# Two layers of gated convolution and MLP, forward and backward: the norm correction one tile behind, and earlier loads in the conv backward

## The chip, the cores and the metric

The kernel runs on one core of one Trainium2 chip. The metric is the device time of one execution in microseconds, less is better. In a profile, PE is TensorE, PEld its weight loads, DVE is VectorE, ACT is ScalarE, POOL is GpSimd and SP is SyncE; a "q" behind the name (SPq, POOLq) is the engine's queue in which it issues DMAs. L1031 is line 1031 of the kernel before.

## The reference

```python
def _A_ref(q, k, v, shift_k, ssm_k, ssm_D):        # gated long convolution
    k_shift = causal 4-tap convolution of k with shift_k
    kv = k_shift * v
    y = irfft(rfft(kv, 2S) * rfft(ssm_k, 2S))[:S]   # long causal convolution, one filter a channel
    return q * (y + kv * ssm_D)

def _B_ref(x, w1, b1, w2, b2):
    return gelu(x @ w1 + b1) @ w2 + b2

x = A_q
x = x + _A_ref(_layernorm(x), A_k, A_v, A_shift_k, A_ssm_k, A_ssm_D)   # layer 0
x = x + _B_ref(_layernorm(x), B_w1, B_b1, B_w2, B_b2)                  # layer 1
x = x + _A_ref(_layernorm(x), ...)                                      # layer 2
x = x + _B_ref(_layernorm(x), ...)                                      # layer 3
# returned: x, and its vjp with grad_out for q, k, v, shift_k, ssm_k, ssm_D, w1, b1, w2, b2
```

S = 2048 tokens, D = 512 channels, F = 1376 hidden units, all arrays in bf16.

## The kernel before, in words

The program has four stages, one behind the other: the conv forward (transforms as matmuls with sine and cosine tables), the MLP forward, the MLP backward, and the conv backward, which is mixed with the weight gradients of the MLP. The norms of the four layers (`n0` to `n3`), the hidden values and their gradients go through DRAM between the stages.

**MLP backward** (`phase_mlp`, `bwd`). The 2048 tokens are four lanes of 512 tokens, each of four token tiles of 128. A lane goes through `b_bwd` (layer 3), `a_bwd` (layer 2), `b_bwd` (layer 1), `a_bwd` (layer 0); so there are eight passes through `b_bwd`. `interleave` writes the four lanes into one program: each `yield` adds to the lane's clock, the lane with the lowest clock goes on, and the lanes start 8 units apart. The framework then places each engine's instructions by its own estimate of when they are ready, with the order of the program as priority; each engine's queue is then worked off strictly in order.

In `b_bwd` a pass first makes `gh = w2T gT` (44 matmuls, L1007), copies it (ScalarE, L1009) and multiplies it with the saved gelu derivative `gpb` (VectorE, L1010). Then for each of four token tiles: 11 matmuls into `gn_ps` (L1023); VectorE sums the product of that tile with the norms into one column (L1026); GpSimd makes a diagonal matrix of the column (L1029); one more matmul adds diagonal times norms to the same PSUM tile (L1031, the correction of the normalisation's backward); VectorE scales and adds the residual gradient to `g_sl` (L1032). The PSUM tile has the tag `oo` with four buffers.

`a_bwd` loads the norms of its own layer (L1044) into a tile of the same tag `n` as `b_bwd` (L1016), of which there are `n_bufs` = 3; then VectorE multiplies norms and gradient (L1053), makes eight sums (L1057, L1059), GpSimd turns these into scales (L1063 to L1066), ScalarE applies them (L1068) and VectorE adds (L1070).

**Conv backward** (`conv_backward`). It is a generator. Each `yield` gives a slack in microseconds, and the main loop puts that much of `weight_grads` (transposes `dw_tp` and matmuls `dw_ps`, sums `b1a` on VectorE) behind it. Everything that the two issue on TensorE and VectorE is kept in the order written (`Ordered`); ScalarE, GpSimd and its DMA queue are placed by the framework. Tiles of a tag reuse its buffers, and a new tile waits for all use of the old one, its stores among it. A pool opened later takes memory of the pools closed before it, and waits for their last use in the same way.

The part that matters begins after the spectra (tag `Sg`, two buffers) have been used: four slices of 512 tokens, each with a load of v (two DMAs, L228) and of ks (L689), two buffers each. For each of four tiles of a slice VectorE multiplies twice, in place: the gradient of v into the ks tile, stored as `out_3` (two DMAs, the second half flipped through `o3B`), and the gradient of the shifted k into `W`. TensorE transposes the latter (`gt_ps`, `gr_ps`), ScalarE copies it to `gksT` and `W[1]`. Then TensorE makes the gradient of k for 16 token tiles (`gk_ps`, 16 matmuls each), ScalarE copies it to `gk_o`, which takes the buffers of v (tag `vb`), four tiles to a store. VectorE makes the gradient of the shift filter: for each of four channel chunks it loads a chunk of k^T (`kTc`, tag `Sg`, L733) and makes eight products with a sum. The next stage, the gradient of the long filter, has matmuls into `gh_ps`, which ScalarE copies to `Wh`.

Of the kernel before, what the change touches and what calls it, by code (L numbers as in the profile page):

```python
# [12 lines left out]
ALU = mybir.AluOpType  # L13
BF16 = mybir.dt.bfloat16
F32 = mybir.dt.float32
I32 = mybir.dt.int32
P = 128
# [606 lines left out]
def conv_backward(ctx, nc, tc, dims, consts, dram, res, aps):  # L624
# [27 lines left out]
    with tc.tile_pool(name="cb_w", bufs=1, side="right", reuse_waits="tile") as wp:  # L652
# [25 lines left out]
        with tc.tile_pool(name="cb_io", bufs=1, side="right", reuse_waits="tile") as io:  # L678
            wdiag = io.tile([P, ND, 4, P], BF16, name="wdiag_b")
            dma(out=wdiag, in_=dram.wdiag)  # L680
            vb0 = io.tile([P, 4, D], BF16, name="vb", tag="vb", bufs=2)
            ksb0 = io.tile([P, 4, D], BF16, name="ksb_b", tag="ksb", bufs=2)
            gT = io.tile([P, ND, S + 16], BF16, name="gksT")
            nc.vector.memset(gT[:, :, S:S + 16], 0.0)
            for i in range(4):
                vb = io.tile([P, 4, D], BF16, name="vb", tag="vb", bufs=2) if i else vb0
                tok_io(nc, vb, v_ap, dram.vB, i, eng=nc.gpsimd)
                ksb = io.tile([P, 4, D], BF16, name="ksb_b", tag="ksb", bufs=2) if i else ksb0
                dma(out=ksb, in_=dram.ks[:, 4 * i:4 * i + 4, :])  # L689
                for h in range(4):  # L690
                    gkv = W[h % 2][:, h // 2, 4 + i, :]
                    tt(out=ksb[:, h, :], in0=gkv, in1=ksb[:, h, :], op=ALU.mult)
                    tt(out=gkv, in0=gkv, in1=vb[:, h, :], op=ALU.mult)
                    ps = psum.tile([P, 2, 512], F32, name="gt_ps", tag="sp", bufs=2)
                    for cc in range(ND):
                        cs = slice(cc * P, (cc + 1) * P)
                        nc.tensor.matmul(ps[:, 0, cs], lhsT=gkv[:, cs], rhs=consts.ident if h < 2 else consts.anti,
                                         start=True, stop=True)
                    if h >= 2:
                        pr = psum.tile([P, 2, 512], F32, name="gr_ps", tag="sp", bufs=2)  # L700
                        for cc in range(ND):
                            cs = slice(cc * P, (cc + 1) * P)
                            nc.tensor.matmul(pr[:, 0, cs], lhsT=gkv[:, cs], rhs=consts.ident, start=True, stop=True)
                        for cc in range(ND):
                            c0 = 256 * (i % 2) + P * (h - 2)
                            nc.scalar.activation(out=W[1][:, cc // 2, 2 * (cc % 2) + i // 2, c0:c0 + P],
                                                 in_=pr[:, 0, cc * P:(cc + 1) * P], func=ACT.Identity)
                    t0 = 512 * i + (P * h if h < 2 else 512 - P * (h - 1))
                    nc.scalar.activation(out=gT[:, :, t0:t0 + P],
                                         in_=ps[:, 0, :].rearrange("p (c t) -> p c t", c=ND), func=ACT.Identity)  # L710
                yield 3.0
                last = tok_io(nc, ksb, out3, dram.o3B, i, store=True, eng=nc.gpsimd)
                if i % 2:
                    with tc.issue_after(last.ins):
                        unflip_rows(nc, aps[f"out_{i // 2}"].flatten_outer_dims(), (dram.o0B, dram.o1B)[i // 2],
                                    eng=nc.gpsimd)
            unflip_rows(nc, out3, dram.o3B, eng=nc.gpsimd)
            for t in range(NT):
                ps = psum.tile([P, 2, 512], F32, name="gk_ps", tag="sp", bufs=2)
                for cc in range(ND):  # L720
                    for j in range(4):
                        nc.tensor.matmul(ps[:, 0, cc * P:(cc + 1) * P], lhsT=gT[:, cc, t * P + j:t * P + j + P],
                                         rhs=wdiag[:, cc, j, :], start=(j == 0), stop=(j == 3))
                if t % 4 == 0:
                    go = io.tile([P, 4, D], BF16, name="gk_o", tag="vb", bufs=2)
                nc.scalar.activation(out=go[:, t % 4, :], in_=ps[:, 0, :], func=ACT.Identity)
                if t % 4 == 3:
                    dma(out=out2[(t - 3) * P:(t + 1) * P, :].rearrange("(t p) d -> p t d", p=P), in_=go)
            gwo = io.tile([P, 2, ND, 4], F32, name="gwo", tag="gwo", bufs=1)
            junk = W[0][:, 0, 0:2, :].rearrange("p a (b d) -> p (a b) d", b=2)  # L730
            for cc in range(ND):
                kc = gyp.tile([P, 8192 // 2], BF16, name="kTc", tag="Sg", bufs=2)[:, 0:4 * 544]
                dma(out=kc, in_=dram.kT[:, cc, :, :].rearrange("p i w -> p (i w)"))  # L733
                kc = kc.rearrange("p (i w) -> p i w", i=4)
                for j in range(4):
                    for half in range(2):
                        if half == 0:
                            g_, k_ = gT[:, cc, 0:S].rearrange("p (i q) -> p i q", i=4)[:, :, 0:256], 16 - j
                        else:
                            g_ = W[1][:, cc // 2, 2 * (cc % 2):2 * (cc % 2) + 2, :].rearrange("p a (b q) -> p (a b) q", b=2)  # L740
                            k_ = 272 + j
                        nc.vector.scalar_tensor_tensor(out=junk, in0=g_, scalar=1.0, in1=kc[:, :, k_:k_ + 256],
                                                       op0=ALU.mult, op1=ALU.mult, accum_out=gwo[:, half, cc, j:j + 1])
                    yield 2.2
            gwb = gyp.tile([P, ND, 4], BF16, name="gwb", tag="gwb", bufs=1)
            tt(out=gwb, in0=gwo[:, 0], in1=gwo[:, 1], op=ALU.add)
# [59 lines left out]
TS = 4  # L806
# [189 lines left out]
def b_bwd(nc, m, g, l, s, ret, rows, load=None):  # L996
# [20 lines left out]
        yield 1.0 * k  # L1017
    go = m.spool.tile([P, TS, D], BF16, name="g_sl", tag=f"x{s}", bufs=1)
    cols = m.small.tile([P, 2, TS], F32, name="bb_cols", tag="bb_cols", bufs=4)
    for t in range(TS):  # L1020
        ps = m.psum.tile([P, D], F32, name="gn_ps", tag="oo", bufs=4)
        for c in range(NFC):
            nc.tensor.matmul(ps, lhsT=gz[:, c, t * P:(t + 1) * P], rhs=w.w1T[:, c, :], start=(c == 0),  # L1023
                             stop=(c == NFC - 1))
        junk = m.small.tile([P, D], BF16, name="bb_junk", tag="bb_junk", bufs=2)
        nc.vector.scalar_tensor_tensor(out=junk, in0=ps, scalar=1.0, in1=n[:, t, :], op0=ALU.mult, op1=ALU.mult,  # L1026
                                       accum_out=cols[:, 0, t:t + 1])
        dg = m.small.tile([P, P], BF16, name="bb_diag", tag="bb_diag", bufs=4)
        nc.gpsimd.tensor_scalar(out=dg, in0=m.ident, scalar1=cols[:, 0, t:t + 1], scalar2=-1.0 / D,  # L1029
                                op0=ALU.mult, op1=ALU.mult)  # L1030
        nc.tensor.matmul(ps, lhsT=dg, rhs=n[:, t, :], start=False, stop=True, skip_group_check=True)  # L1031
        nc.vector.scalar_tensor_tensor(out=go[:, t, :], in0=ps, scalar=m.rstd[l][:, s * TS + t:s * TS + t + 1],  # L1032
                                       in1=g[:, t, :], op0=ALU.mult, op1=ALU.add, accum_out=cols[:, 1, t:t + 1])
        yield 2.5
    ret.append((go, cols[:, 1, :]))


def a_bwd(nc, m, g, sumg, l, s, go, first, ret):
    D = m.D
    sl = slice(s * TS, (s + 1) * TS)  # L1040
    y = m.y[:, sl, :]
    rstd = m.rstd[l][:, sl]
    n = m.spool.tile([P, TS, D], BF16, name="nb_sl", tag="n", bufs=m.n_bufs)
    nc.sync.dma_start(out=n, in_=tok(m.n_d[l], s))  # L1044
    u = m.gpool.tile([P, TS, D], BF16, name="ab_u", tag="ab_u", bufs=2)
    for t in range(TS):
        nc.scalar.activation(out=u[:, t, :], in_=y[:, t, :], func=ACT.Identity, scale=rstd[:, t:t + 1],
# [152 lines left out]
def phase_mlp(ctx, nc, tc, dims, consts, dram, res, aps):  # L1200
# [11 lines left out]
    with ExitStack() as st:  # L1212
# [2 lines left out]
        m.spool = st.enter_context(tc.tile_pool(name="m_s", bufs=1))  # L1215
        m.hpool = st.enter_context(tc.tile_pool(name="m_h", bufs=1))
        m.psum = st.enter_context(tc.tile_pool(name="m_ps", bufs=1, space=bass.MemoryType.PSUM, reuse_waits="tile"))
        m.n_bufs = 3
        m.mhalf = m.small.tile([P, TS], F32, name="mhalf", bufs=1)
        nc.vector.memset(m.mhalf, -0.5)  # L1220
        with tc.tile_pool(name="m_g", bufs=2, reuse_waits="tile") as m.gpool:
# [20 lines left out]
        with tc.tile_pool(name="m_gb", bufs=2, reuse_waits="tile") as m.gpool:  # L1242

            def bwd(s):
# [1 line left out]
                g3 = G3[:, s * TS:(s + 1) * TS, :]  # L1246
                yield from b_bwd(nc, m, g3, 3, s, ret, dram_rows(go_ap, dram.goB, s),
                                 lambda: tok_io(nc, g3, go_ap, dram.goB, s))
                g, sg = ret.pop()
                yield from a_bwd(nc, m, g, sg, 2, s, G1[:, s * TS:(s + 1) * TS, :], True, ret)  # L1250
                ret.pop()
                g1 = G1[:, s * TS:(s + 1) * TS, :]
                yield from b_bwd(nc, m, g1, 1, s, ret, sb_rows(g1))
                g, sg = ret.pop()
                yield from a_bwd(nc, m, g, sg, 0, s, None, False, ret)
                tok_io(nc, ret.pop(), out1, dram.o1B, s, store=True)

            interleave([(s * 8.0, bwd(s)) for s in range(NSL)])
# [66 lines left out]
```

## Time and profile before

| | |
|---|---|
| median of 3 runs | 1016.43 us (1014.85 to 1016.79) |
| profiled execution | 1015.93 us |
| its span in the profile | 1013.8 us, 12809 instructions |
| granted TensorE clock, mean | 0.918 |
| DMA | 177.72 MB, mean 175 GB/s |

Times inside the profile count from the start of the span. Rows of "waits" say which engine and line waited for whom: in total, how often, the longest. Rows in order of time give start, duration, engine, line, operation, output <- input, the count, and in brackets the idle time of the engine ahead of it with what ended it. L55 is the line of the helper that keeps the written order, so there the tile's name says which operation it is. In rows of stretches each engine has its busy time and count, followed by the granted TensorE clock, the mean busy share of the 16 DMA engines, and GB/s.

### The profile page before, as it was taken

What the parts mean: (1) busy time and instruction counts of PE and PEld (TensorE: products, weight loads), DVE (VectorE), ACT (ScalarE), POOL (GpSimd) and SP (SyncE); (2) the same over time, 40 slices, a digit from 0 to 9 for tenths busy, and PEclk for the clock granted to TensorE, in tenths of its full rate; (3) what the DMA queues carried; (4) which work ended last, traced back from release to release, by engine and by line L of the source; (5) the groups of instructions that cost most, each with busy time, mean ns of one, the idle gap of its engine ahead of it and who ended that gap; (6) DMA issues with size and microseconds to landing.
All of it is one profiled execution on the core that took longest, in us unless ns stands there. A gap on an engine that the chain in (4) does not pass through costs nothing.

```text
span 1013.8 us, 12809 instructions
## 1 busy us (share of the span) xinstructions
PE 807.2 (80%) x4677; PEld 411.5 (41%) x4754; DVE 733.2 (72%) x1207; ACT 612.5 (60%) x806; POOL 150.5 (15%) x271
## 2 busy tenths in 40 slices
PE   0678768872777678768998988879899995879998
PEld 0444333340323233323433333335355553655674
DVE  6615529597999999977466567885369993897883
ACT  5735435452889988889724444535465654645664
POOL 5411100002212221100011111221010203310000
PEclk9788979986889898879999999989999998879999
DMA  5076637204365445685895767448256588656231
GB/s 207 22 267 203 259 124 260 83 1 145 112 189 151 131 139 156 200 231 160 265 280 176 214 175 168 146 161 296 109 165 237 200 310 278 186 166 199 89 107 44
DMA packets 153415, 177.72 MB, mean 175 GB/s; under 512 B 50117, under 2 KB 133768, under 8 KB 152712
## 3 DMA queue, kind: packets, MB, share of 16 engines
q1 hardware_dynamic: 141816, 136.75, 43.7%
q0 software_dynamic: 11536, 40.15, 11.0%
q8 instruction: 37, 0.61, 0.3%
q14 instruction: 26, 0.21, 0.1%
HBM read 92.61 MB, written 82.13 MB: 172 GB/s over the span
## 4 chain that ended last, share of the span: by engine, by line
PE 28%; DVE 19%; DMA 11%; ACT 8%; issue 6%; POOL 4%; SPq 1%; ACTq 0%; DVEq 0%; POOLq 0%
PE dw_ps L55 10%; DMA nb_sl<-n_d 3%; DVE ln_st L891 3%; PE gh_ps L1007 3%; PE sp_ps L55 2%; PE dw_tp L55 2%; PE gh_ps L55 2%; PE iv_ps L55 2%; DMA ksb_b<-ks_d 2%; PE gn_ps L1023 2%; DVE g_o L961 2%; DMA tabFb<-tabF_d 2%; POOL bb_diag L1029 2%; DVE bb_junk L1057 2%; ACT g_o L957 1%
## 5 line engine op out<-in xcount | busy, mean ns | idle before, releaser
L55 PE MATMUL dw_ps<-G,dw_tm 128*128 128x512 bf16 x672 | 166.9, 383 | 3.1 <-ACT dw_tm L1121 1.4
L1121 ACT ACTIVATE dw_tm<-dw_tp 128x1024 bf16<-128x1024 bf16 x88 | 89.9, 1024 | 68.3 <-PE dw_tp L55 68.2
L990 PE MATMUL o_ps<-w_sb,h_sl 128*128 128x512 bf16 x343 | 95.7, 422 | 39.9 <-DVE h_sl L960 39.0
L978 PE MATMUL z_ps<-nT_sl,w_sb 128*128 128x512 bf16 x346 | 83.1, 394 | 20.4 <-DMA nT_sl<-n_sl 18.6
L55 PEld LDWEIGHTS <-dw_tm 128*128 128x128 bf16 x704 | 65.3, 99 | 62.2 <-ACT dw_tm L1121 2.1
L1009 ACT ACTIVATE gz_sl<-gh_ps 128x512 bf16<-128x512 f32 x88 | 51.2, 597 | 60.2 <-PE gh_ps L1007 59.2
L1023 PE MATMUL gn_ps<-w1T_sb,gz_sl 128*128 128x512 bf16 x346 | 82.8, 386 | 1.3 <-DVE gz_sl L1010 0.9
L1007 PE MATMUL gh_ps<-gT_sl,w2T_sb 128*128 128x512 bf16 x343 | 82.1, 383 | 0.4
L990 PEld LDWEIGHTS <-h_sl 128*128 128x128 bf16 x352 | 36.4, 107 | 92.9 <-DVE h_sl L960 45.1
L978 PEld LDWEIGHTS <-w_sb 128*128 128x128 bf16 x352 | 35.0, 101 | 73.0 <-DMA nT_sl<-n_sl 27.9
L980 ACT ACTIVATE g_z<-z_ps,b1col 128x512 bf16<-128x512 f32 x88 | 54.1, 690 | 11.3 <-PE z_ps L978 11.3
L55 PEld LDWEIGHTS <-dw_fm 128*128 128x128 bf16 x704 | 48.2, 100 | 21.1 <-issue 1.4
L55 PE MATMUL dw_tp<-ident,dw_fm 128*128 128x128 bf16 x704 | 55.3, 223 | 0.0
L956 ACT ACTIVATE g_s<-g_t 128x2048 bf16<-128x2048 bf16 (+1 forms) x24 | 42.5, 1773 | 18.3 <-DVE g_t L955 18.3
L1023 PEld LDWEIGHTS <-gz_sl 128*128 128x128 bf16 x352 | 34.9, 100 | 43.4 <-issue 3.5
L1007 PEld LDWEIGHTS <-w2T_sb 128*128 128x128 bf16 x352 | 34.6, 98 | 40.3 <-issue 0.8
L55 DVE TENSOR_REDUCE b1a<-dw_fm 128x1 f32<-128x2048 bf16 x22 | 49.6, 2279 | 1.0 <-DMA dw_fm<-gz_d 1.0
L1029 POOL TENSOR_SCALAR bb_diag<-ident,bb_cols 128x128 bf16<-128x128 bf16 x32 | 22.9, 716 | 157.8 <-DVE bb_junk L1026 156.5
L894 POOL TENSOR_SCALAR rstd<-ln_mv 128x4 f32<-128x4 f32 x16 | 11.5, 717 | 232.9 <-DVE ln_mv L892 148.8
L1010 DVE TENSOR_TENSOR gz_sl<-gz_sl,gpb 128x2048 bf16<-128x2048 bf16 (+1 forms) x24 | 27.2, 1135 | 24.3 <-ACT gz_sl L1009 13.5
L1068 ACT ACTIVATE nb_sl<-nb_sl,ab_ab 128x512 bf16<-128x512 bf16 x32 | 24.6, 804 | 33.1 <-DVE bb_junk L1026 22.9
L891 DVE BATCH_NORM_STATS2 ln_st<-x_sl 128x6 f32<-128x512 bf16 x64 | 41.9, 668 | 2.9 <-DMA x_sl<-in_A_q_dram 2.8
(284 smaller groups left out, 1646.0 us busy)
## 6 DMA issues: line engine op xcount, KB each, us to landing
dw_fm<-h_d SPq DMA_DIRECT2D x22, 512.0 KB, 5.1
dw_fm<-gz_d SPq DMA_DIRECT2D x22, 512.0 KB, 4.5
n_d<-n_sl SPq DMA_DIRECT2D x16, 512.0 KB, 3.5
h_d<-h_sl SPq DMA_DIRECT2D x16, 512.0 KB, 2.9
gp_d<-g_p SPq DMA_DIRECT2D x16, 512.0 KB, 3.5
nb_sl<-n_d SPq DMA_DIRECT2D x16, 512.0 KB, 4.6
gpb<-gp_d SPq DMA_DIRECT2D x16, 512.0 KB, 4.8
gz_d<-gz_sl SPq DMA_DIRECT2D x16, 512.0 KB, 4.9
```

Of the source, the lines that this page charges most:

```text
L55: return self.tc.keep_in_program_order(f(*args, **kwargs))
L891: nc.vector.bn_stats(out=st, in_=x[:, t, :])
L956: nc.scalar.activation(out=sg, in_=t, func=ACT.Sigmoid)
L978: nc.tensor.matmul(ps, lhsT=w.w1[:, dc, c * P:(c + 1) * P], rhs=nT[:, dc, :], start=(dc == 0), stop=(dc == ND - 1))
L980: nc.scalar.activation(out=zb[:, c - c0, :], in_=ps, func=ACT.Identity, bias=w.b1col[:, c:c + 1])
L990: nc.tensor.matmul(ps, lhsT=h[:, c, t * P:(t + 1) * P], rhs=w.w2[:, c, :], start=False, stop=(c == NFC - 1))
L1007: nc.tensor.matmul(ps, lhsT=w.w2T[:, dc, c * P:(c + 1) * P], rhs=gT[:, dc, :], start=(dc == 0), stop=(dc == ND - 1))
L1009: nc.scalar.activation(out=gz[:, c, :], in_=ps, func=ACT.Identity)
L1010: nc.vector.tensor_tensor(out=gz[:, c0:c0 + k, :], in0=gz[:, c0:c0 + k, :], in1=gp[:, 0:k, :], op=ALU.mult)
L1023: nc.tensor.matmul(ps, lhsT=gz[:, c, t * P:(t + 1) * P], rhs=w.w1T[:, c, :], start=(c == 0), stop=(c == NFC - 1))
L1029: nc.gpsimd.tensor_scalar(out=dg, in0=m.ident, scalar1=cols[:, 0, t:t + 1], scalar2=-1.0 / D, op0=ALU.mult, op1=ALU.mult)
L1121: nc.scalar.activation(out=dst, in_=ps, func=ACT.Identity)
```

## The change

1. In `b_bwd` the loop over token tiles has one more round. In round t the 11 matmuls of tile t come first, then the correction matmul and `g_sl` of tile t-1, then the sum and the diagonal of tile t. In round 1 `b_bwd` also issues the load of the norms that the following `a_bwd` needs and hands the tile over; `a_bwd` loads nothing. `n_bufs` in the MLP is 4 instead of 3.
2. In the conv backward all four slices' ks and v loads are issued ahead of the slice loop: ks into four buffers, v into two tiles of two slices each in the buffers of the spectra (tag `Sg`). The output tiles of the k gradient take the ks buffers (four) instead of the v buffers (two).
3. All four chunks of k^T are loaded ahead of the matmuls of the k gradient: two into the `Sg` buffers, which hold v until then, and two into parts of `W[0]`.

```diff
@@ conv_backward
-            vb0 = io.tile([P, 4, D], BF16, name="vb", tag="vb", bufs=2)
-            ksb0 = io.tile([P, 4, D], BF16, name="ksb_b", tag="ksb", bufs=2)
+            ksbs = [io.tile([P, 4, D], BF16, name="ksb_b", tag="ksb", bufs=4) for i in range(4)]
+            vbs = []
+            for i in range(4):
+                if i % 2 == 0:
+                    v2 = gyp.tile([P, 2, 4, D], BF16, name="vb", tag="Sg", bufs=2)
+                vbs.append(v2[:, i % 2])
+                dma(out=ksbs[i], in_=dram.ks[:, 4 * i:4 * i + 4, :])
+                tok_io(nc, vbs[i], v_ap, dram.vB, i, eng=nc.gpsimd)
...
             for i in range(4):
-                vb = io.tile([P, 4, D], BF16, name="vb", tag="vb", bufs=2) if i else vb0
-                tok_io(nc, vb, v_ap, dram.vB, i, eng=nc.gpsimd)
-                ksb = io.tile([P, 4, D], BF16, name="ksb_b", tag="ksb", bufs=2) if i else ksb0
-                dma(out=ksb, in_=dram.ks[:, 4 * i:4 * i + 4, :])
+                vb, ksb = vbs[i], ksbs[i]
...
+            w0f = W[0][:, :, :, :].rearrange("p e s d -> p (e s d)")
+            kcs = [gyp.tile([P, 4096], BF16, name="kTc", tag="Sg", bufs=2)[:, 0:4 * 544] for cc in range(2)]
+            kcs += [w0f[:, 2048 + 2176 * x:2048 + 2176 * (x + 1)] for x in range(2)]
+            for cc in range(ND):
+                dma(out=kcs[cc], in_=dram.kT[:, cc, :, :].rearrange("p i w -> p (i w)"))
             unflip_rows(nc, out3, dram.o3B, eng=nc.gpsimd)
...
-                    go = io.tile([P, 4, D], BF16, name="gk_o", tag="vb", bufs=2)
+                    go = io.tile([P, 4, D], BF16, name="gk_o", tag="ksb", bufs=4)
...
-                kc = gyp.tile([P, 8192 // 2], BF16, name="kTc", tag="Sg", bufs=2)[:, 0:4 * 544]
-                dma(out=kc, in_=dram.kT[:, cc, :, :].rearrange("p i w -> p (i w)"))
-                kc = kc.rearrange("p (i w) -> p i w", i=4)
+                kc = kcs[cc].rearrange("p (i w) -> p i w", i=4)
@@ b_bwd
-    for t in range(TS):
-        (11 matmuls; sum; diagonal; correction; g_sl of tile t, as above)
-        yield 2.5
-    ret.append((go, cols[:, 1, :]))
+    pss = {}
+    for t in range(TS + 1):
+        if t < TS:
+            (11 matmuls of tile t into pss[t])
+        if t > 0:
+            u, ps = t - 1, pss.pop(t - 1)
+            nc.tensor.matmul(ps, lhsT=dg, rhs=n[:, u, :], start=False, stop=True, skip_group_check=True)
+            (g_sl of tile u)
+        if t < TS:
+            (sum and diagonal dg of tile t)
+        if t == 1:
+            n2 = m.spool.tile([P, TS, D], BF16, name="nb_sl", tag="n", bufs=m.n_bufs)
+            nc.sync.dma_start(out=n2, in_=tok(m.n_d[l - 1], s))
+        yield 2.5 if t < TS else 0.2
+    ret.append((go, cols[:, 1, :], n2))
@@ a_bwd
-    n = m.spool.tile([P, TS, D], BF16, name="nb_sl", tag="n", bufs=m.n_bufs)
-    nc.sync.dma_start(out=n, in_=tok(m.n_d[l], s))
@@ phase_mlp
-        m.n_bufs = 3
+        m.n_bufs = 4
```

More of the change, by code (lines that the diff above doesn't have):

```diff
@@ L1019, in b_bwd @@
     cols = m.small.tile([P, 2, TS], F32, name="bb_cols", tag="bb_cols", bufs=4)
-    for t in range(TS):
[L1021 to L1033, printed above, removed]
-        yield 2.5
@@ L1035, in b_bwd @@
-    ret.append((go, cols[:, 1, :]))
-def a_bwd(nc, m, g, sumg, l, s, go, first, ret):
+    pss = {}
+    for t in range(TS + 1):
+        if t < TS:
+            ps = pss[t] = m.psum.tile([P, D], F32, name="gn_ps", tag="oo", bufs=4)
+            for c in range(NFC):
+                nc.tensor.matmul(ps, lhsT=gz[:, c, t * P:(t + 1) * P], rhs=w.w1T[:, c, :], start=(c == 0),
+                                 stop=(c == NFC - 1))
+        if t > 0:
+            u, ps = t - 1, pss.pop(t - 1)
+            nc.tensor.matmul(ps, lhsT=dg, rhs=n[:, u, :], start=False, stop=True, skip_group_check=True)
+            nc.vector.scalar_tensor_tensor(out=go[:, u, :], in0=ps, scalar=m.rstd[l][:, s * TS + u:s * TS + u + 1],
+                                           in1=g[:, u, :], op0=ALU.mult, op1=ALU.add, accum_out=cols[:, 1, u:u + 1])
+        if t < TS:
+            junk = m.small.tile([P, D], BF16, name="bb_junk", tag="bb_junk", bufs=2)
+            nc.vector.scalar_tensor_tensor(out=junk, in0=pss[t], scalar=1.0, in1=n[:, t, :], op0=ALU.mult,
+                                           op1=ALU.mult, accum_out=cols[:, 0, t:t + 1])
+            dg = m.small.tile([P, P], BF16, name="bb_diag", tag="bb_diag", bufs=4)
+            nc.gpsimd.tensor_scalar(out=dg, in0=m.ident, scalar1=cols[:, 0, t:t + 1], scalar2=-1.0 / D,
+                                    op0=ALU.mult, op1=ALU.mult)
+        if t == 1:
+            n2 = m.spool.tile([P, TS, D], BF16, name="nb_sl", tag="n", bufs=m.n_bufs)
+            nc.sync.dma_start(out=n2, in_=tok(m.n_d[l - 1], s))
+        yield 2.5 if t < TS else 0.2
@@ L1039, in a_bwd @@
+    ret.append((go, cols[:, 1, :], n2))
+def a_bwd(nc, m, g, sumg, n, l, s, go, first, ret):
     D = m.D
@@ L1248, in bwd @@
                                  lambda: tok_io(nc, g3, go_ap, dram.goB, s))
-                g, sg = ret.pop()
-                yield from a_bwd(nc, m, g, sg, 2, s, G1[:, s * TS:(s + 1) * TS, :], True, ret)
+                g, sg, n = ret.pop()
+                yield from a_bwd(nc, m, g, sg, n, 2, s, G1[:, s * TS:(s + 1) * TS, :], True, ret)
                 ret.pop()
@@ L1253, in bwd @@
                 yield from b_bwd(nc, m, g1, 1, s, ret, sb_rows(g1))
-                g, sg = ret.pop()
-                yield from a_bwd(nc, m, g, sg, 0, s, None, False, ret)
+                g, sg, n = ret.pop()
+                yield from a_bwd(nc, m, g, sg, n, 0, s, None, False, ret)
                 tok_io(nc, ret.pop(), out1, dram.o1B, s, store=True)
```

## The prediction

> **What bounds the kernel now.** I read the page first (busy shares and the 40 slices of 25.3 us), then busy time by stage, then the waits of the stages that the diff touches, and last the order of time in them.
>
> ```profile
> PE 807.2 (80%) x4677; PEld 411.5 (41%) x4754; DVE 733.2 (72%) x1207; ACT 612.5 (60%) x806; POOL 150.5 (15%) x271
> PE   0678768872777678768998988879899995879998
> DVE  6615529597999999977466567885369993897883
> ```
>
> ```profile
> core 0: us, PE busy (x) PEld busy (x) DVE busy (x) ACT busy (x) POOL busy (x), PEclk, DMA share, GB/s
> 495.00:680.00 185.00, 159.12 (x694) 67.56 (x706) 128.90 (x285) 85.77 (x137) 29.44 (x60) 0.97 0.70 201
> ...
> 806.00:870.00 64.00, 50.46 (x378) 29.80 (x384) 44.58 (x65) 34.72 (x63) 15.26 (x22) 0.89 0.80 270
> 870.00:902.00 32.00, 22.93 (x306) 20.77 (x308) 30.20 (x39) 15.21 (x31) 6.55 (x8) 0.84 0.51 161
> 902.00:930.00 28.00, 27.79 (x214) 16.22 (x216) 26.53 (x36) 16.14 (x19) 3.31 (x4) 1.00 0.79 247
> 930.00:1013.00 83.00, 77.89 (x608) 51.71 (x614) 53.30 (x80) 49.12 (x79) 3.71 (x6) 1.00 0.28 84
> ```
>
> TensorE is the engine to watch in all of them. The backward MLP runs from about 495 to 680 us: TensorE idles 25.9 us there and VectorE 56.1. In the conv backward, 806 to 870 and 870 to 902 hold 13.5 and 9.1 us of idle TensorE; 902 to 930 is full, and 930 to the end 94% full. From 806 on TensorE and VectorE run in an order written into the program, and that order is the same after the change. So idle time taken from TensorE there comes off the end, unless VectorE then ends last.
>
> **Part 1: the correction one token tile behind.** The waits between 495 and 697 us (total, times, longest) name the idle time:
>
> ```profile
> PE gn_ps L1031 <- POOL bb_diag L1029: 23.8, 23, 3.4
> ...
> DVE g_sl L1032 <- PE gn_ps L1031: 22.3, 26, 1.5
> ...
> DVE gy_bf L1053 <- DMA nb_sl<-n_d: 7.8, 4, 3.2
> ```
>
> Nearly all of TensorE's idle time, 23.8 of 25.9 us, is before the correction matmul, which needs the VectorE sum of the same token tile and then the GpSimd diagonal. VectorE in turn waits 22.3 us for that matmul. One pass in order of time shows how the two feed each other:
>
> ```profile
> 574.95 0.39 PE L1031 MATMUL gn_ps<-nb_sl,bb_diag 128*128 128x512 bf16 x1 [0.18 <-POOL bb_diag L1029]
> ...
> 575.37 0.95 SPq L1044 DMA_DIRECT2D nb_sl<-n_d  x1
> ...
> 582.47 1.23 DVE L1053 TENSOR_TENSOR gy_bf<-nb_sl,g_sl 128x2048 bf16<-128x2048 bf16 x1 [3.21 <-DMA nb_sl<-n_d]
> ...
> 586.18 0.68 DVE L1026 SCALAR_TENSOR_TENSOR bb_junk<-gn_ps,nb_sl 128x512 bf16<-128x512 f32 x1
> ...
> 586.97 1.02 POOL L1029 TENSOR_SCALAR bb_diag<-ident,bb_cols 128x128 bf16<-128x128 bf16 x1
> ...
> 588.04 0.61 PE L1031 MATMUL gn_ps<-nb_sl,bb_diag 128*128 128x512 bf16 x1 [3.38 <-POOL bb_diag L1029]
> ```
>
> The norms of the next stage are asked for right behind the pass's last correction (574.95 + 0.39, issue at 575.37): that buffer became free only then. They land 7 us later, VectorE stands 3.21 us for them, its queue (the sum at 586.18 among it) is late, and TensorE stands 3.38 us.
>
> After the change the eleven matmuls of the next tile stand between a tile's product and its correction:
>
> ```profile
> 542.81 2.39 PE gn_ps L1023 x11
> ```
>
> The way from sum to correction is 588.04 - 586.18 = 1.86 us in the pass above, where GpSimd took 1.02 us. It fits behind 2.39 us as long as VectorE isn't over 0.5 us late. No instruction is added on TensorE, VectorE or GpSimd; 32 corrections, sums and diagonals move. The last tile of each of eight passes has no own product behind it and relies on other lanes' matmuls; in the last pass there are none. The norm loads keep their number (SyncE, 16 in all) and move from behind the last correction to the second tile, some two tiles or 5 us earlier. SyncE issues in order, so a load that waits for a buffer holds up the transposes and gpb loads behind it. Followed by hand through the interleaved lanes, four buffers give each second-stage load a free slot within about one token tile's time of when it is issued; the first-stage loads wait for the same releases as now. The fourth buffer pays for the earlier load; I cost the queue at nothing, and if it isn't covered it is a rival below.
>
> Bounds: nothing, if the waits only move, and 23.8 us. Below nothing needs a new wait, which is the slower rival. VectorE allows the gain: 22.3 + 7.8 us of its 56.1 idle are these waits. But in the last third it is nearly full (645 to 670 us: 21.0 of 25), so the ends of passes stay. I take 15 us, about two thirds, nearer to the upper row because the chain of 1.9 us is shorter than its new cover.
>
> **Part 2: v, ks and k^T at once.** TensorE and VectorE in order of time:
>
> ```profile
> 850.84 0.59 PE L55 MATMUL dw_ps<-G,dw_tm 128*128 128x512 bf16 x2
> 860.57 0.61 PE L55 MATMUL gt_ps<-ident,Wb 128*128 128x128 bf16 x4 [9.14 <-DVE Wb L55]
> ...
> 868.93 0.61 PE L55 MATMUL gt_ps<-ident,Wb 128*128 128x128 bf16 x8
> ...
> 875.25 9.10 PE L55 MATMUL gk_ps<-wdiag_b,gksT 128*128 128x128 bf16 x160
> 892.70 8.26 PE L55 MATMUL gk_ps<-wdiag_b,gksT 128*128 128x128 bf16 x96 [8.36 <-ACT gk_o L726]
> ```
>
> ```profile
> 859.63 0.42 DVE L55 TENSOR_TENSOR ksb_b<-Wb,ksb_b 128x512 bf16<-128x512 bf16 x1 [16.71 <-DMA ksb_b<-ks_d]
> ...
> 870.48 1.23 DVE L55 SCALAR_TENSOR_TENSOR Wb<-gksT,kTc 128x1024 bf16<-128x1024 bf16 x1 [2.20 <-ACT gksT L709]
> ...
> 926.41 1.23 DVE L55 SCALAR_TENSOR_TENSOR Wb<-Wb,kTc 128x1024 bf16<-128x1024 bf16 x1
> ```
>
> ```profile
> 795.47 0.56 POOL L733 DMA_DIRECT2D kTc<-kT_d  x1 [6.49 <-DVE pr_u L55]
> ...
> 844.58 0.58 POOL L689 DMA_DIRECT2D ksb_b<-ks_d  x1 [1.61 <-DMA o3B_d<-ksb_b]
> ```
>
> ```profile
> 892.06 1.09 ACT L726 ACTIVATE gk_o<-gk_ps 128x512 bf16<-128x512 f32 x2 [8.87 <-DMA out_dram<-gk_o]
> ...
> 935.70 1.09 ACT L780 ACTIVATE Wh<-gh_ps 128x514 bf16<-128x514 f32 x2
> ```
>
> Two gaps go. *Slice 2:* its ks load waits for slice 0's store to land and is issued at 844.58; VectorE waits 16.71 us, TensorE 9.14. With four ks buffers it is issued with the first ones. *The k gradient:* the third output tile waits for the first one's store; TensorE idles 8.36. With four buffers, free once the slices' own stores have landed, this goes too.
>
> The clock adds to it. In stretches of 5 us (columns as above; PEclk is third from the end):
>
> ```profile
> 820.00:825.00 5.00, 4.95 (x37) 2.76 (x36) 4.90 (x7) 2.55 (x3) 0.00 (x0) 1.00 0.47 129
> ...
> 855.00:860.00 5.00, 0.00 (x0) 0.00 (x0) 0.37 (x1) 0.00 (x0) 0.00 (x0) 0.50 0.26 102
> 860.00:865.00 5.00, 3.75 (x26) 2.57 (x27) 4.86 (x9) 3.31 (x10) 1.43 (x2) 0.50 0.39 136
> ...
> 890.00:895.00 5.00, 2.30 (x22) 2.29 (x22) 4.90 (x8) 1.48 (x3) 0.00 (x0) 0.50 0.22 90
> ```
>
> The granted clock is 0.50 after each gap. The last 96 matmuls took 8.26 us; at the rate of the first 160 (9.10 / 160) they take 5.46, so 2.8 us are lost. After the first gap I put 1.7 us: two groups of four transposes took 0.61 each where later one group of eight did, and the gradient matmuls between slices 2 and 3 are slow too. TensorE: 9.14 + 8.36 + 2.8 + 1.7 = 22.0 us. The Trainium skill ("TensorE: Matmul & The Clock Gate", Part 1) agrees on the half clock after an idle window, but has it last about 3.4 us, which would make 1.7 us lost per gap, an estimate 1.1 us under my two terms; the rows decide.
>
> VectorE caps this. It is full from 870 to 930 us, and its shift-filter products read the transposed gradient that TensorE makes in slice 3. That slice starts 868.93 - (9.14 + about 1.4 of clock) = 858.4, so VectorE moves by 10.5 us, not 16.7. Its last product, at 926.41, ends 9.3 - 1.2 = 8.1 us before ScalarE fills the next stage's buffer at 935.70, which I assume lies over that gradient. So the path moves by at most 10.5 + 8.1 = 18.6 us before VectorE ends last, less than 22.0: I take 18.6.
>
> Costs: eight v and four ks loads are only moved in GpSimd's queue. The last load would be issued near 810, instead of 849, and nothing in that queue is due until the first store at 835.8. The DMA must carry 1 MB of ks more before 834; the half-free stretch 820 to 825 (share 0.47) has room for most of it. The Trainium skill ("DMA: Bandwidth & Descriptors", Issuing engines are not separate DMA queues) speaks against a gain from issuing at once: all loads share the same engines. Here the four slices are due 6 us and more apart from 834 on, so sharing costs nothing unless the landing passes 834. k^T loses its early start: its first two loads, now at 795.47 and later, get the buffers that then hold v, so the first can start after slice 1 (about 841) and at worst behind slice 3's stores (about 856). First use is near 860, landings are 4 to 9 us; that costs VectorE 0 to 5 us. I take 2, nearer to the free end since GpSimd is idle after slice 1's stores.
>
> Sum: 15 + 18.6 - 2 = 31.6 us. The profiled execution took 1015.93 us (span 1013.8 and 2.1 around it), 0.5 under the median of 1016.43. 1015.93 - 31.6 = 984.3.
>
> **The rivals.**
> (A) Both parts pay: 984, from 976 to 992 (MLP part 10 to 20, conv part 14 to 19).
> (B) The MLP part pays little: VectorE has 128.9 of 185 us of work in a fixed queue, and a correction that comes later makes the next stage's input later too; the waits move to the sums or to the gz products. With 3 us left of it: 996. For it speaks the dense last third; against it 22.3 + 7.8 us of VectorE waits that have nothing to wait for any more.
> (C) The conv loads pay half: the k^T loads or the stores land late (DMA share near 1.0 around 830 to 850), and VectorE, already full, carries the delay. With 9 us of conv gain: 992.
> (D) Slower: product tiles are held over one more tile, and there are four PSUM buffers for lanes that overlap in pairs; three live tiles a lane would be six. A product that waits for another lane's correction and g_sl costs at least 0.39 + 0.75 us. From 1.0 us on each of 32 tiles it eats the whole 31.6; at 1.5 us the time is 1032, counted as 1015.93 - 31.6 + 48. Against it: no wait of a product for a PSUM buffer stands among today's waits.
> (E) No change: the gaps go, but all move to VectorE's end: 1016.
>
> **How the numbers follow.** A 0.56, B 0.19, C 0.12, D 0.06, E 0.03; 0.04 for more than expected, under 976. The prediction is A's 984. From 973 to 1001 the range leaves out D, E and edges, together about 0.15. A, B, C and the upside are faster: 0.91 less 0.01 for a B that shrinks to nothing. Within 0.2%, which is about what a measurement of this kernel can tell from no change, 0.03; slower 0.07.
>
> **What would show it.** Right: TensorE's wait for the diagonal under 9 us in total; second-stage norm loads issued before the pass's last correction, and no VectorE wait for them; no VectorE wait for ks; 256 k-gradient matmuls in one run of about 14.6 us; the next filter stage 17 us closer to the start of the conv backward. Wrong: a wait of the products for a PSUM tile, of VectorE for k^T, or of TensorE for the norms.

## The result, and the profile after

Median 985.06 us (982.26 to 987.2, four runs) against 1016.61 us for the kernel before (1014.85 to 1021.69, four runs): ratio 0.968, 95% interval 0.9638 to 0.9722. The forecast of 984 is met within 1.1 us, but the two terms behind it are not: the MLP part paid far more than its 15 us and the conv part about half of its 16.6, and the errors cancelled. The profiled execution took 987.2 us, span 985.4.

From the page of the changed kernel, TensorE's row and the 40 slices (of 24.6 us):

```profile
PE 803.6 (82%) x4677; PEld 411.7 (42%) x4754; DVE 729.5 (74%) x1207; ACT 611.6 (62%) x806; POOL 152.5 (15%) x271
...
PE   0686867984378777777899999978999998995998
...
DVE  6624508787899999995847778895369997499873
```

The work is the same (803.6 us of TensorE against 807.2, with equal counts) in a span 28.4 us shorter. Four marks show where it went: the first `gpb` load, the first sine-table matmul (`sp_ps`, right behind the MLP backward), VectorE's first product on `ks`, and the end.

| us | start of MLP backward | its length | middle stage | conv part |
|---|---|---|---|---|
| before | 490.5 | 223.8 | 120.0 | 179.5 |
| after | 496.75 | 198.9 | 118.8 | 171.0 |

The start lies 6 us later although nothing ahead of it was changed; over all kernels below it lies between 489.6 and 498.8, so I count it as chance and compare lengths of stages. They say 25 us in the MLP and 8.5 in the conv part.

**The MLP part.** Busy time by stretches, from the first `gpb` load to the last correction and to the first sine-table matmul (columns: TensorE, its weight loads, VectorE, ScalarE, GpSimd, then clock, DMA share, GB/s). Before:

```profile
490.50:678.10 187.60, 161.72 (x700) 67.97 (x712) 127.24 (x282) 89.12 (x143) 29.44 (x60) 0.98 0.70 203
490.50:714.30 223.80, 191.18 (x902) 84.81 (x917) 146.79 (x312) 107.01 (x163) 34.38 (x67) 0.97 0.71 214
```

After:

```profile
496.75:660.90 164.15, 154.81 (x701) 69.27 (x713) 124.94 (x283) 88.05 (x143) 31.81 (x60) 0.98 0.79 230
496.75:695.60 198.85, 184.84 (x902) 86.42 (x917) 143.35 (x312) 106.05 (x163) 36.74 (x67) 0.97 0.78 238
```

Waits of the changed kernel from 495 to 680 us (total, times, longest):

```profile
DVE g_sl L1036 <- PE gn_ps L1035: 11.7, 6, 3.0
...
DVE gz_sl L1016 <- DMA gpb<-gp_d: 11.4, 5, 5.3
...
PE gn_ps L1035 <- POOL bb_diag L1043: 8.3, 5, 4.0
```

TensorE's wait for the diagonal fell from 23.8 us in 23 waits to 8.3 in 5; two of these five, 2.81 and 4.03 us in the last pass, hold 6.8 of it. No row of VectorE waiting for the norms is left.

And TensorE is *busy* 6.9 us less for the same 700 matmuls (161.72 to 154.81). A part of that is the clock. Before, a wait of 2.72 us that ended at 559.74 and the one of 3.38 us that ended at 588.04 were followed by half clock while TensorE worked without a pause:

```profile
560.50:562.50 2.00, 2.00 (x7) 0.75 (x5) 1.68 (x5) 2.00 (x4) 0.00 (x0) 0.52 0.12 42
588.50:590.50 2.00, 2.00 (x6) 0.70 (x5) 1.81 (x5) 0.99 (x3) 0.00 (x0) 0.50 0.90 268
```

Counting half of the busy time at clock 0.50 as lost, an estimate, the stretch lost 3.5 us to the clock before and 0.9 after. That is 2.7 of the 6.9 us. The other 4.2 are 0.23 us for each of the 18 waits that went, over the wait itself; what makes them up was not tried.

**The conv part.** GpSimd's queue, VectorE, ScalarE and TensorE of the changed kernel in order of time:

```profile
832.92 1.67 POOL L219 DMA_DIRECT2D out_dram<-o1B_d  x1 [0.81 <-issue]
834.58 1.13 POOL L724 DMA_DIRECT2D kTc<-kT_d  x2
840.10 1.05 POOL L724 DMA_DIRECT2D Wb<-kT_d  x2 [4.39 <-PE gt_ps L55]
```

```profile
830.68 0.42 DVE L55 TENSOR_TENSOR ksb_b<-Wb,ksb_b 128x512 bf16<-128x512 bf16 x1
...
850.61 1.23 DVE L55 SCALAR_TENSOR_TENSOR Wb<-gksT,kTc 128x1024 bf16<-128x1024 bf16 x1 [19.05 <-DMA kTc<-kT_d]
...
903.42 1.22 DVE L55 SCALAR_TENSOR_TENSOR Wb<-gksT,Wb 128x1024 bf16<-128x1024 bf16 x1
...
904.69 1.22 DVE L55 SCALAR_TENSOR_TENSOR Wb<-Wb,Wb 128x1024 bf16<-128x1024 bf16 x1
```

```profile
904.74 1.09 ACT L786 ACTIVATE Wh<-gh_ps 128x514 bf16<-128x514 f32 x2 [9.95 <-DVE Wb L55]
```

```profile
845.50 14.46 PE L55 MATMUL gk_ps<-wdiag_b,gksT 128*128 128x128 bf16 x256
...
905.39 8.03 PE L55 MATMUL gh_ps<-tabG,GY 128*128 128x257 bf16 x48 [10.30 <-ACT Wh L786]
```

Both old gaps are gone: no wait for ks, and the 256 matmuls of the k gradient run in one piece of 14.46 us. But k^T is asked for at 834.58, behind all stores of the slices, and is there at 850.61. VectorE stands 19.05 us. The last of its products that reads the transposed gradient in `gksT` is the last but one, at 903.42; ScalarE fills `Wh` as soon as that has ended, at 904.74, and TensorE stands 10.30 us for ScalarE. The 48 matmuls behind that gap take 8.03 us; before, behind a gap of 0.25 us, they took 5.51.

### The profile page after: what moved, and what is told of

It is laid out like the page before. It is cut to its first block, busy times and chain, and to the rows that moved or that the text cites. A ratio compares the mean times of both kernels' runs of the same rounds, so it can differ in the third digit from the quotient of the medians.

```text
span 985.4 us, 12825 instructions
## 1 busy us (share of the span) xinstructions
PE 803.6 (82%) x4677; PEld 411.7 (42%) x4754; DVE 729.5 (74%) x1207; ACT 611.6 (62%) x806; POOL 152.5 (15%) x271
## 4 chain that ended last, share of the span: by engine, by line
PE 38%; DVE 35%; ACT 9%; DMA 7%; issue 5%; POOL 4%; SPq 1%; ACTq 0%; DVEq 0%; POOLq 0%
PE sp_ps L55 8%; PE gh_ps L1013 6%; PE gn_ps L1031 6%; DVE Wb L55 6%; PE dw_ps L55 5%; DVE ln_st L897 3%; PE gh_ps L55 3%; DVE b1a L55 2%; DVE g_o L967 2%; PE iv_ps L55 2%; DMA Hspec_d<-Hg 2%; DMA kTc<-kT_d 2%; DMA tabFb<-tabF_d 2%; DVE pr_u L55 2%; PE dw_tp L55 1%
## 5 line engine op out<-in xcount | busy, mean ns | idle before, releaser
L1031 PE MATMUL gn_ps<-w1T_sb,gz_sl 128*128 128x512 bf16 x345 | 80.7, 379 | 0.6 <-DVE gz_sl L1016 0.3
L1013 PE MATMUL gh_ps<-gT_sl,w2T_sb 128*128 128x512 bf16 x344 | 79.1, 379 | 0.5
L959 ACT ACTIVATE g_q<-g_z 128x2048 bf16<-128x2048 bf16 (+1 forms) x24 | 42.8, 1783 | 0.1
```

The lines of the kernel that those rows point to most:

```text
L959: nc.scalar.activation(out=q, in_=zb, func=ACT.Square)
L1013: nc.tensor.matmul(ps, lhsT=w.w2T[:, dc, c * P:(c + 1) * P], rhs=gT[:, dc, :], start=(dc == 0), stop=(dc == ND - 1))
```

## The experiments

All times are medians; each ratio is to the kernel before, run on the same chip. The three stages are read at the marks of the table above.

**1 and 2: each part by itself.** The first takes `b_bwd`, `a_bwd` and `n_bufs` from the change and `conv_backward` from before; the second the reverse.

> The MLP part alone; the conv backward is as before. Theory (the waits for the diagonal were the whole idle time of that stage and they go): from the first gpb load to the first transform matmul of the conv backward the trace went from 223.8 to 198.9 us, so 1016.5 - 25 = 991.5 us, with TensorE's gaps of 9.1 and 8.4 us in the conv backward back. Rival (the prediction's size, 15 us, and the rest of the trace's difference belongs to the conv part or to chance): 1001 us.

Measured: 992.84 us, ratio 0.9781 [0.9731, 0.983]; MLP backward 199.9, conv part 178.6.

> The conv part alone; the MLP is as before. Theory (the late k^T loads cost most of what the loads and buffers gain): from the first ks product to the end the trace went from 179.5 to 171.0 us, so 1016.5 - 8.5 = 1008 us, VectorE waiting some 19 us for k^T. Rival (the prediction's size, 16.6 us): 1000 us, no wait for k^T above 5 us.

Measured: 1008.15 us, ratio 0.9911 [0.9876, 0.9945]; MLP backward 222.7, conv part 170.4. In its waits VectorE again stands 19.0 us for k^T and TensorE 11.9 for `Wh`:

```profile
DVE Wb L55 <- DMA kTc<-kT_d: 19.0, 1, 19.0
PE gh_ps L55 <- ACT Wh L786: 11.9, 1, 11.9
ACT Wh L786 <- DVE Wb L55: 11.6, 1, 11.6
```

The two parts are independent: 2.2% and 0.9% add up to about the 3.2% of both, and each stage's length in the change is that of the part alone, within 1.1 us.

**3: k^T early.** Three chunks go into the buffer of the output gradient, which is free by then, ahead of the slices.

```diff
+            gyf = res.gy_bf[:, :, :].rearrange("p t d -> p (t d)")
+            kcs = [gyf[:, 2176 * x:2176 * (x + 1)] for x in range(3)] + [w0f[:, 4224:6400]]
+            for cc in range(3):
+                dma(out=kcs[cc], in_=dram.kT[:, cc, :, :].rearrange("p i w -> p (i w)"))
             for i in range(4):          # the slices
...
+            dma(out=kcs[3], in_=dram.kT[:, 3, :, :].rearrange("p i w -> p (i w)"))
```

> The changed kernel with three chunks of k^T loaded ahead of the slices into the buffer of the input gradient (free after the inverse transform), the fourth into W behind slice 3. Theory (VectorE starts the shift filter 8 us late only because of k^T, and its end sets the next stage): VectorE's wait for k^T goes from 19 to about 10 us (then it waits for the transposed gradient), TensorE's gap of 10.3 us before the next stage shrinks to about 2, and the half clock behind it goes: 985 - 10 = 975 us. Rival (the loads come when the DMA is full, so they push others back, or VectorE is bound anyway): 983 us or more.

Measured: 972.31 us (971.17 to 976.52), ratio 0.9579 [0.9539, 0.9618], below the interval of the change. The conv part took 157.6 us, 13.5 less than in the change and 21.9 less than before. Its VectorE, ScalarE and TensorE in order of time:

```profile
836.70 1.23 DVE L55 SCALAR_TENSOR_TENSOR Wb<-gksT,gy_bf 128x1024 bf16<-128x1024 bf16 x1 [7.48 <-ACT gksT L717]
...
891.44 1.22 DVE L55 SCALAR_TENSOR_TENSOR Wb<-Wb,Wb 128x1024 bf16<-128x1024 bf16 x1
```

```profile
891.49 1.09 ACT L787 ACTIVATE Wh<-gh_ps 128x514 bf16<-128x514 f32 x2 [0.73 <-DVE Wb L55]
```

```profile
892.14 5.51 PE L55 MATMUL gh_ps<-tabG,GY 128*128 128x257 bf16 x48 [1.08 <-ACT Wh L787]
```

VectorE now waits for the transposed gradient only, TensorE stands 1.08 us instead of 10.30, and the 48 matmuls are back at 5.51.

**4: ks, v and the output buffers without the k^T loads.** k^T is loaded inside the loop of products, as before, but its `Sg` buffers hold v.

> Conv part without the early k^T: ks and v at once, four output buffers, k^T chunk by chunk as before (two buffers, which now hold v until slice 1 and slice 3 are done); MLP as before. Theory (k^T is late because its buffers hold v and its loads stand behind other DMAs; asking for it in the loop makes it later still): slower than the conv part alone by 0 to 6 us, 1008 to 1014 us. Rival (k^T's place doesn't matter, the gain comes from ks and the output buffers): the same as the conv part alone within 2 us.

Measured: 1024.89 us, ratio 1.0104 [1.0039, 1.0169]; conv part 184.8. It was expected to stay faster than the kernel before and is slower. GpSimd's queue, VectorE's wait, and the stretches behind:

```profile
879.06 0.75 POOL L731 DMA_DIRECT2D out_dram<-gk_o  x1 [2.82 <-ACT gk_o L729]
879.81 1.10 POOL L736 DMA_DIRECT2D kTc<-kT_d  x2
```

```profile
DVE Wb L55 <- DMA kTc<-kT_d: 33.7, 1, 33.7
```

```profile
915.00:930.00 15.00, 7.22 (x50) 4.29 (x51) 14.62 (x21) 3.56 (x4) 2.36 (x3) 0.76 0.82 257
930.00:945.00 15.00, 6.41 (x39) 4.61 (x37) 14.83 (x19) 2.96 (x6) 0.78 (x1) 0.56 0.26 62
```

The load that went out at 795.47 before now stands behind the fourth store of the k gradient. VectorE idles 33.7 us beside work of TensorE and then makes its 32 products; from 915 us on TensorE is half idle beside them. So the freed buffers alone lose; they need k^T moved with them.

**7: only the first chunk early.** As experiment 3, with chunk 0 alone ahead of the slices.

> The changed kernel with the first chunk of k^T alone loaded ahead of the four slices (into the output gradient's buffer, which is free by then); the other three chunks are issued where they were. With three chunks ahead the time was 972.3 us. Theory (only the first chunk's landing at 850.6 us costs, VectorE standing 19 us for it; the later chunks land while the first is multiplied for 9.8 us): VectorE's products begin within 1 us of the transposes' end at about 842, the conv part from the first ks product takes 157 to 160 us, total 971 to 975 us. Rival (the queue is as long for the second chunk: it still lands 15 to 17 us after its issue and VectorE stands for it after the first): a new wait of 3 to 9 us for the second chunk, conv part 162 to 167, total 977 to 982 us.

Measured: 975.69 us, ratio 0.9551 [0.9512, 0.959]; conv part 157.7, as with three chunks. VectorE's first product:

```profile
842.02 1.23 DVE L55 SCALAR_TENSOR_TENSOR Wb<-gksT,gy_bf 128x1024 bf16<-128x1024 bf16 x1 [7.53 <-ACT gksT L714]
```

No wait for the second chunk follows, though it still took 15.4 us from issue to landing. Only the first landing was on the path.

**8: what makes the landing slow.** In the changed kernel, two memory-to-memory copies of 1 MB (the reversed rows of `out_1` and `out_3`) go behind the second and fourth store of the k gradient.

```diff
-                if i % 2:
+                if i == 1:
                     with tc.issue_after(last.ins):
                         unflip_rows(...)
...
-            unflip_rows(nc, out3, dram.o3B, eng=nc.gpsimd)
...
+                    if t in (7, 15):
+                        with tc.issue_after(last.ins):
+                            (unflip_rows of out_1 at t = 7, of out3 at t = 15)
```

> The changed kernel with two memory-to-memory copies, the reversed rows of out_1 and of the third output (1 MB each), moved behind the second and the fourth store of gk; the k^T loads keep their place behind slice 3's stores. Theory (k^T lands 16 us after its issue because those copies fill the DMA engines that it shares): the first chunk lands 6 to 10 us after its issue, VectorE waits 6 to 11 us for it instead of 19, conv part 161 to 165 us against 171, total 975 to 980 us. Rival (the stores of the slices and the other stage's loads alone keep the engines full): landing 14 us or more, VectorE waits 15 us or more, total 983 to 987 us.

Measured: 978.28 us, ratio 0.9572 [0.9522, 0.9622]; conv part 163.6. The issue and the first product:

```profile
833.37 1.12 POOL L724 DMA_DIRECT2D kTc<-kT_d  x2
```

```profile
844.84 1.23 DVE L55 SCALAR_TENSOR_TENSOR Wb<-gksT,kTc 128x1024 bf16<-128x1024 bf16 x1 [12.01 <-DMA kTc<-kT_d]
```

The two `Sg` loads landed 11.8 us after issue (median) instead of 16.4, which is still later than the 6 to 10 us expected, and VectorE's wait is 1 us above its range; conv part and total lie in theirs. In experiment 4 the same loads, issued when little else ran, took 4.7 (median of four). So the traffic beside them sets the landing, the copies some 4.6 us of it; how the rest divides between the slices' stores and the other stage's loads was not tried. Of the 13.5 us of conv part between the change and experiment 3, 7.4 go with the copies; how the other 6.1 divide between the late issue and the other traffic was not tried either. This split rests on one profiled execution of each kernel: the ratios of experiments 3 and 8 (0.9579 and 0.9572) do not tell the two apart.

**5: the lag alone.** Round loop of the change, norms loaded in `a_bwd` as before, three buffers, conv part as before.

> The kernel before with the lag alone: the correction's diagonal matmul and the add run one token tile behind, norms loaded where they were (three buffers), convolution backward as before. MLP stage alone with both parts took 199.9 us from the first gpb load to the first sine-table matmul, 223.8 before. Theory (the lag covers the waits of TensorE for the diagonal and is most of the gain): stage 204 to 209 us, TensorE's wait for the diagonal below 10 us against 23, VectorE's wait for the norms still 7 to 12 us, total 998 to 1003 us. Rival (the two parts need each other: without the diagonal's wait the kernel only comes earlier to norms that are not there): VectorE's wait for the norms grows to 15 us or more, stage 213 or more, total 1008 us.

Measured: 1022.51 us, ratio 1.004 [1.0013, 1.0068]; MLP backward 231.8 in the profiled execution, 8 us *more* than before. That execution took 1028.16 us, the longest of ten; the ratio puts the loss at some 4 us (1.3 to 6.9). The rival named the wait that grows, but its 1008 us was too low. The waits from 495 to 680 us, and one pass in order of time:

```profile
PE gn_ps L1029 <- POOL bb_diag L1037: 23.8, 6, 8.3
DVE gy_bf L1058 <- DMA nb_sl<-n_d: 17.7, 4, 7.6
...
DVE ab_p L1058 <- DMA nb_sl<-n_d: 4.0, 2, 3.4
```

```profile
533.08 0.38 PE L1029 MATMUL gn_ps<-nb_sl,bb_diag 128*128 128x512 bf16 x1
...
535.21 0.41 SPq L1049 DMA_DIRECT2D nb_sl<-n_d  x1
...
541.88 1.22 DVE L1058 TENSOR_TENSOR gy_bf<-nb_sl,g_sl 128x2048 bf16<-128x2048 bf16 x1 [7.63 <-DMA nb_sl<-n_d]
...
545.60 0.68 DVE L1034 SCALAR_TENSOR_TENSOR bb_junk<-gn_ps,nb_sl 128x512 bf16<-128x512 f32 x1
...
546.46 0.37 POOL L1037 TENSOR_SCALAR bb_diag<-ident,bb_cols 128x128 bf16<-128x128 bf16 x1 [0.19 <-DVE bb_junk L1034]
...
546.89 0.61 PE L1029 MATMUL gn_ps<-nb_sl,bb_diag 128*128 128x512 bf16 x1 [8.26 <-POOL bb_diag L1037]
```

The last correction at 533.08 frees the norms' buffer, the next norms are asked for at 535.21 and used at 541.88; VectorE stands 7.63 us for them. In its queue the other lane's sum (545.60) lies behind, so that lane's diagonal is late and TensorE stands 8.26 us. A lag of one tile, 2.4 us, cannot cover that. It also makes the last correction later, and so the load: the total wait for norms from 495 to 680 us rose from 9.4 to 21.7 us.

Up to the last correction of the stage TensorE waits 31.7 us for the diagonal, in eight waits only; before it was 23.8 in 23. The stretch:

```profile
496.30:693.40 197.10, 164.52 (x715) 71.11 (x713) 126.53 (x283) 89.55 (x143) 25.64 (x60) 0.92 0.68 195
```

With a third of the waits TensorE is busier than before (161.72), at a clock of 0.92 instead of 0.98. By the estimate used above, 9.2 us of this stretch are lost to half clock, and the rest, 155.3, lies close to that of the change (154.0). So a few long waits cost more here than many short ones.

**6: the norms alone.** Loaded a stage ahead, four buffers, correction in its old place.

> The kernel before with the norms alone: loaded a stage ahead into four buffers, correction in its old place, convolution backward as before. Theory (two separate waits, the norms' being the smaller): VectorE's wait for the norms goes, TensorE's wait for the diagonal stays at 20 us or more, stage 215 to 219 us against 223.8, total 1008 to 1012 us. Rival (the norms' wait is covered by the diagonal's, and is worth nothing by itself): stage 222 or more, total 1015 to 1018 us.

Measured: 1013.45 us, ratio 0.9944 [0.9916, 0.9971]; MLP backward 219.7, 4 us less than before. Its waits from 495 to 680 us:

```profile
DVE g_sl L1032 <- PE gn_ps L1031: 22.5, 27, 1.0
PE gn_ps L1031 <- POOL bb_diag L1029: 21.0, 24, 2.6
```

Norms are never waited for, and the short way from sum to diagonal to correction stays open on 26 of 32 tiles (23.8 us up to the last correction at 683.42). So the waits before had two sources: the short way behind most tiles, and a load in another lane behind some long ones. In stage lengths of the profiled executions the lag alone costs 8 us and the early norms alone bring 4; together they bring 24 (experiment 1). By the ratios it is 0.4% slower, 0.6% faster and 2.2% faster.

**9 and 10: the place or the buffer.** Experiment 5 with `n_bufs` 4, the loads left in `a_bwd`; and the changed kernel with `n_bufs` 3.

> The kernel before with the lag and a fourth norms buffer; the loads stay at the head of the second stage, convolution backward as before. The lag alone took 231.8 us for the MLP stage, with VectorE waiting 21.7 us for norms whose load goes out only once the pass's last correction, now a tile later, has released its buffer. Theory (the buffer's release is what makes that load late): with a free buffer the load goes out before the last correction, VectorE's wait for the norms falls under 6 us, TensorE's for the diagonal under 12, stage 200 to 208 us, total 992 to 1001 us. Rival (the load's place counts: SyncE takes it up only behind the pass's other issues): VectorE still waits 12 us or more, stage 215 or more, total 1008 us or more.

Measured: 992.4 us, ratio 0.9779 [0.9705, 0.9852]; MLP backward 199.7. Its waits before the correction, for the sum and for the diagonal, and the second of its loads beside its use:

```profile
PE gn_ps L1029 <- DVE bb_junk L1034: 4.3, 4, 2.8
...
PE gn_ps L1029 <- POOL bb_diag L1037: 4.0, 1, 4.0
```

Together these are 8.3 us in five waits, as in the change.

```profile
539.48 0.36 SPq L1049 DMA_DIRECT2D nb_sl<-n_d  x1
...
548.92 1.22 DVE L1058 TENSOR_TENSOR gy_bf<-nb_sl,g_sl 128x2048 bf16<-128x2048 bf16 x1
```

> The changed kernel with three norms buffers in place of four; all else as changed (985.06 us, MLP stage 198.9 us). Theory (the early load lives from the fourth buffer: with three it stands in SyncE's queue until the pass's last correction releases one, and holds up the gpb loads and transposes behind it): the loads go out behind the last correction, VectorE waits 12 us or more for norms and gpb together more than now, stage 215 to 235 us, total 1001 to 1021 us. Rival (the place alone does it, the buffer is free in time anyway): stage 198 to 204 us, total 984 to 991 us.

Measured: 987.2 us, ratio 0.9718 [0.9645, 0.9791]; MLP backward 199.4. The theory was wrong here, the rival right:

```profile
536.71 0.36 SPq L1047 DMA_DIRECT2D nb_sl<-n_d  x1
...
546.15 1.22 DVE L1065 TENSOR_TENSOR gy_bf<-nb_sl,g_sl 128x2048 bf16<-128x2048 bf16 x1
```

In both the load goes out 9.4 us ahead of its use and VectorE does not stand for it; over the whole stage VectorE waits 0.8 us for norms in experiment 10 and not at all in experiment 9. Either the fourth buffer or the earlier place does it; the change has both and needs one.

## Why the prediction was right, and where its sum was not

**MLP part, 15 us: undersized; 25 measured (24 with this part alone).** The mechanism was the one named: TensorE's wait for the diagonal fell to 8.3 us (forecast under 9), VectorE's for the norms went, and no product waits for a PSUM tile, so rival D did not come. "About two thirds" of the 23.8 us came out as well: 15.5 went. The step that failed is that the term counts these waits and nothing else. Up to the last correction TensorE idles 16.5 us less and is busy 6.9 us less, and behind it another 1.5 us went (TensorE's wait for the sine table fell from 5.2 to 1.3 us, that for `dw_tm` rose from 1.4 to 3.0); these make up the 25. The prediction counted the half clock behind the gaps of part 2 and put it at nothing in part 1, and the upper bound of 23.8 leaves out the busy time in the same way. That "the ends of passes stay" held for the last pass only, which has 6.8 of the 8.3 us. "The fourth buffer pays for the earlier load" did not hold either: three pay for it as well.

Costing the norms' load as a side term was right only by luck. It was the condition: without it the lag loses some 4 us by the ratio and 8 in the profiled stage. The prediction's own pass showed it (a load at 575.37 right behind the correction, VectorE and then TensorE standing), but the sum put TensorE's wait down to the short way from sum to correction.

**Conv part, 18.6 less 2 for k^T: oversized; 8.5 measured.** The failed step is the 2 us. "At worst behind slice 3's stores" is what happened, and the landing, taken as 4 to 9 us, was 16.4. VectorE's wait for k^T was one of the prediction's own signs of being wrong, and it came. VectorE's first filter product starts 36.2 us after the first ks product (850.61 - 814.39), as before (870.48 - 834.32): the 10.5 us by which it was to move were lost whole. What is left is the slack behind VectorE. It was 9.3 us and not 8.1, because ScalarE waits for the last product over `gksT` and not for the very last one; and VectorE's row of products got 1.8 us shorter. So `Wh` comes 11.0 us closer to the first ks product (90.4 us instead of 101.4; forecast 17), and the half clock behind the new gap takes 2.5 us of that back. Rival C described this; its price of 9 us of conv gain was nearly exact, and it had a chance of 0.12.

With k^T in time (experiment 3) the conv part gained 21.9 us: TensorE idles 17.0 us less than before and is busy 4.9 less, where the prediction had 17.5 of gaps and 4.5 of clock. So TensorE's sum of 22.0 us was right, and the cap of 18.6 was 3.3 too low: the first product came 11.5 us earlier (at 24.65) instead of 10.5, the slack was 9.3, and VectorE's row got 1.2 us shorter. That `Wh` lies over the transposed gradient, which was assumed, agrees with ScalarE's start at 904.74, right behind the product over `gksT` that ran from 903.42.

**The sum.** 24.9 + 8.5 and 1.2 in the middle stage are 34.6 us between the profiled executions, of which the later start of the MLP took back 6.2: 28.4 net. The medians say 31.6, which is the prediction's sum; a reader should not take that for a confirmation of its terms.

**The clock.** The prediction put 2.8 and 1.7 us on the half clock behind two gaps. Behind the new gap it cost 2.5 us (8.03 against 5.51): the clock was 0.50 from 905 to 910 us and 0.93 from 910 to 915. In experiment 8, behind a gap of 4.93 us, it cost 2.2 (7.70); behind 1.08 us nothing. The Trainium skill ("TensorE: Matmul & The Clock Gate", Part 1) gives some 3.4 us of half clock, which makes 1.7 us lost, an estimate; these rows lie 0.5 to 0.8 above.

## What to carry to other kernels

A wait that is named after one engine may have its source in another lane: follow it back through the in-order queue to the load that holds the queue, since a software lag of one tile covers a short chain and not a load. When pricing a wait, look at the clock of the rows behind it too: the term for the waits came out here, and the busy time that went with them was left out. Where buffers are freed to move loads earlier, ask what loses its early start for it, and give the first piece of that a place of its own: one chunk of 0.5 MB early was worth as much as three. Estimate the landing of a load from what else moves in that stretch.

## What the runs showed of the hardware

The same k^T loads of 544 KB landed in 4.7, 11.8 and 16.4 us (experiment 4, experiment 8, the change), by what moved beside them. The Trainium skill ("DMA: Bandwidth & Descriptors", Issuing engines are not separate DMA queues) says that all loads interleave on the same 16 engines whichever engine starts them. The three landings fit that, but do not test it: the copies that experiment 8 moved were issued from GpSimd's queue, like k^T itself.

A wait of TensorE can cost more than it lasts. Waits of 2.72 and 3.38 us in the MLP backward before were followed by half clock (0.52 and 0.50), waits of up to 1.82 us in the same stage were not (1.00 behind that one). Waits of 10.30 and 4.93 us in the conv backward were followed by 48 matmuls in 8.03 and 7.70 us, one of 1.08 us (experiment 3) by the same 48 in 5.51. What share of a short wait's cost is not the clock, 0.23 us a wait by the estimate above, was not split further.
